# A planner's condition on the first layer's output weights, and new draws for its order

## The chip, the cores and the metric

The kernel runs on one core of one Trainium2 chip. The metric is device time in microseconds (us); the kernel before takes 1172.25 us as the median of 3 runs (1171.01 to 1172.92). The core has five engines that run their own instruction streams side by side: PE (TensorE, matmuls), DVE (VectorE), ACT (ScalarE), POOL (GpSimd) and SP (SyncE), which here issues the DMA transfers.

## The reference

Three steps follow one another: attention with pooled keys and values, a first layer with a softmax gate and a normalisation, and a second layer with a sigmoid gate. The inputs arrive as float64 words.

```python
k_p = k.reshape(B, H, Sp, pool, D).mean(axis=3)      # B = H = 8, S = 576, D = 64, pool = 8
v_p = v.reshape(B, H, Sp, pool, D).mean(axis=3)
attn = softmax(scale * q @ k_p.T)
x = (attn @ v_p) as (4608, 512)

h = x @ w_in                                         # 512 -> 1024
solu = h * softmax(h)
ln = (solu - mean(solu)) / sqrt(var(solu) + 1e-06) * g_ln
y = ln @ w_out                                       # 1024 -> 512

h = y @ w2_in                                        # 512 -> 2048
out = (h * sigmoid(1.702 * h)) @ w2_out              # 2048 -> 512
```

## The kernel before

The work has two phases. The first runs from the start to about 517 us: attention and the first layer over 36 tiles of 128 tokens, and besides, in the gaps, the preparation of all weights. The second phase, the remaining 652 us, is the second layer over 6 blocks of 768 tokens; its order is written out by hand.

In the first phase a planner (class `Plan`) sets the order. Each piece of work is a strand, a generator that yields operations (`Op`), requests for a tile (`New`) or conditions (a function that must give true before the strand goes on). In `Plan.run` the planner looks at the next operation of each strand, estimates when it could begin on its engine, adds a term from the strand's due time and a random number times a size, and emits the operation with the lowest score. `DRAWS` (line 85) lists up to which planned PE time which size and which seed hold. So one random stream decides between operations that are nearly equally good, and once one choice differs, all later draws meet other candidates. The emitted order is fixed at build time. Each engine executes its instructions in that order and waits at each for its inputs.

The strands that matter here:

- `w_in_part` (684) and `w_in_scale` (703): the four quarters of w_in are loaded (1 MB each, float64), their maximum is taken on DVE (tile `w1i_am`), spread over the partitions with a small matmul (`largest`, 566), and a power-of-two scale is computed from it (`whole_scale`, 645). Then `first_half` (670) writes each piece as a high half (ACT) and a low half (DVE) into `w1i`. The spread of an early scale uses the PSUM bank `psy`, of which there is one, shared with the pooled keys and values (`pooled`, 790) and with the projection.
- `second_weight` (718): w_out in four parts (`part`, 731). Each takes one of the 4 `raw` tiles, loads 1 MB, is joined to float32 (`joined`, 655: a sign and a scaling on ACT, a shift-and-or on DVE, a product on POOL) and measured (tile `w1o_am`). When all four are measured, the scale follows, and then the halves into `w1o`. The strands of w_in's last two quarters take their `raw` tiles first, so w_out's parts 2 and 3 wait until those give theirs back.
- `attention` (857): for each tile the scores (`psx`), softmax, and the softmax weights as high and low halves in `st`. A DMA transpose turns them into `aT`. For the first 4 tiles (`ALONE`) each transpose is issued by itself; `turned[t]` is set right after the planner has emitted it (lines 914 to 920). Then comes the product with the values (bank `psv`, of which there is one), and its halves go to `xT`.
- `Pair.hidden` (962): the product with w_in into `psh` (two buffers), its maximum, exponential, and the product with it (tile `tt`), which releases the buffer. `Pair.norm` (1008) ends with a DMA transpose into `zT`, and `Pair.project` (1050) multiplies with `w1o`.
- `Quarter` (1083) and `unit_scale` (1154): the second layer's weights, prepared in the same way in the gaps, from the time when the third tile's hidden product has been planned.

All loads, stores and transposes of this phase go through SP's queue, in the planner's order. An instruction there that waits for its input holds back those behind it.

Of the kernel before, what the change touches and what calls it, by code (L numbers as in the profile page):

```python
# [81 lines left out]
LATE = 3000  # L82
LATE_TURN = 3000
TTS = 4
DRAWS = ((70e3, 600, 13), (200e3, 150, 4), (330e3, 150, 13), (1e9, 150, 1))
V_TOP = 2.0 ** 14

TOP3 = 2.0 ** -29 * (1 - 2.0 ** -23)
# [95 lines left out]
class Plan:  # L184
# [7 lines left out]
    def __init__(self):  # L192
        self.free = dict.fromkeys(("pe", "dve", "act", "pool", "sp", "dma", "none"), 0.0)
        self.uses, self.floor, self.rings, self.ring_of = {}, {}, {}, {}
        self.strands, self.now, self.warm, self.pool_from = [], None, 0.0, 0.0
        self.draws = [(until, size, random.Random(seed)) for until, size, seed in DRAWS]

    def start(self, steps, due):
        s = Strand(self, steps, due)
        self.strands.append(s)  # L200
        return s
# [14 lines left out]
    def drop(self, *tiles):  # L216
        for t in tiles:
            del self.ring_of[t.name]
# [78 lines left out]
def moe_kernel(ctx: ExitStack, tc: tile.TileContext, qT, kT, vT, w_in, w_out, g_ln, w2_in, w2_out, eye, outT):  # L297
# [66 lines left out]
    class Tokens:  # L364
# [26 lines left out]
        def largest(self, diag):  # L391

            am = t1("yam")
            nc.vector.tensor_reduce(out=am, in_=self.two, axis=AX.X, op=ALU.max)
            nc.vector.tensor_scalar(out=diag, in0=eye_t, scalar1=am, scalar2=TINY, op0=ALU.mult, op1=ALU.max)
            self.diag = diag
# [39 lines left out]
    with ExitStack() as ph:  # L436
# [22 lines left out]
        def until(*strands):  # L459
            return lambda: all(s.ended for s in strands)  # L460
# [50 lines left out]
        def V(name, *args, **kw):  # L511
            return op(("dve",), name, args, kw)
# [47 lines left out]
        def s1(name, n=1, bufs=2):  # L560
            return small.tile([P, n], F32, name=name, tag=name, bufs=bufs)

        def absmax_op(dst, src, axis=AX.X):
            return V("tensor_reduce", out=dst, in_=src, axis=axis, op=ALU.max, apply_absolute_value=True)
# [68 lines left out]
        def raw_new(q, n):  # L633
            return New(kv, [P, q, n, 2], I32, "raw", "raw", RAWS)

        def raw_load(raw, src, i, n, q):
            return D(
                raw.rearrange("p q f t -> p q (f t)"),
                src[i * q * P : (i + 1) * q * P, :].bitcast(I32).rearrange("(q p) f -> p q f", p=P),
            )  # L640

        def high_words(raw):
            return raw[:, :, :, 1].bitcast(F32)

        def whole_scale(alln, up, dn):

            pw, rc = s1("pw", 1, KM), s1("rc", 1, KM)
            yield from exponent(pw, alln)
            yield V("reciprocal", rc, pw)
            yield V("tensor_scalar_mul", rc, rc, rc)  # L650
            yield V("tensor_scalar_mul", rc, rc, rc)
            yield V("tensor_scalar", out=up, in0=rc, scalar1=rc, scalar2=2.0 ** 8, op0=ALU.mult, op1=ALU.mult)
            yield V("reciprocal", dn, up)

        def joined(raw, measured):

            hw, lw = raw[:, :, 1], raw[:, :, 0]
            sg = yield New(kv, [P, 2 * WC], F16, "sgw", bufs=SG // 2)
            yield A(out=sg, in_=hw.bitcast(F32), func=AF.Sign)
            yield A(out=lw.bitcast(U32), in_=lw.bitcast(U32), func=AF.Copy, scale=TOP3, bias=-0.49999)  # L660
            yield measured
            yield A(out=hw.bitcast(F32), in_=hw.bitcast(F32), func=AF.Copy, scale=2.0 ** -112)
            yield V(
                "scalar_tensor_tensor", out=lw, in0=hw, scalar=3, in1=lw, op0=ALU.logical_shift_left,
                op1=ALU.bitwise_or,
            )
            yield G("tensor_tensor", out=lw.bitcast(F32), in0=sg, in1=lw.bitcast(F32), op=ALU.mult)
            drop(sg)

        def first_half(join, raw, scaled, up, k, c, his):  # L670

            yield join.over
            yield scaled
            word = raw[:, :, 0].bitcast(F32)
            hi, lo = (x[:, k, c] for x in his)
            yield A(out=hi, in_=word, func=AF.Copy, scale=up)
            yield V("scalar_tensor_tensor", out=lo, in0=word, scalar=up, in1=hi, op0=ALU.mult, op1=ALU.subtract)
# [40 lines left out]
        def second_weight(due):  # L718
            n = 4
            am, a1, alln, gs = s1("w1o_am", n), s1("w1o_a1"), s1("w1o_all"), s1("w1o_gs", K1)  # L720
            measured = [None] * n

            def scale():
                yield lambda: all(measured)
                yield V("tensor_reduce", out=a1, in_=am, axis=AX.X, op=ALU.max)
                yield from largest(a1, alln, WIDE_LEAST)
                yield from whole_scale(alln, w1o_up, w1o_dn)
                yield g_done.over
                yield V("tensor_scalar_mul", gs, g_col, w1o_up)

            def part(i):
                raw = yield raw_new(2, DM)
                yield raw_load(raw, w_out, i, DM, 2)
                join = start(joined(raw.rearrange("p q f t -> p (q f) t"), lambda: measured[i]), due + 4 * i)
                two = [
                    start(
                        first_half(
                            join, raw[:, j], scaled.over, gs[:, 2 * i + j : 2 * i + j + 1], 2 * i + j,
                            slice(0, WC), w1o,
                        ),  # L740
                        due + 4 * i,
                    )
                    for j in range(2)
                ]

                def measure():
                    yield absmax_op(am[:, i : i + 1], high_words(raw), axis=AX.XY)
                    measured[i] = True

                start(measure(), DUE_MAX_OUT)  # L750
                yield until(*two)
                drop(raw)

            scaled = start(scale(), due)
            yield until(*[start(part(i), due + 4 * i) for i in range(n)])

        BY_PRODUCT = (1, 2)
# [513 lines left out]
        q_loaded, scored, turned, valued, hid = ([False] * NTILE for _ in range(5))  # L1271
# [453 lines left out]
```

## Time and profile before

| | value |
|---|---|
| median of 3 runs | 1172.25 us |
| lowest, highest | 1171.01, 1172.92 us |
| the profiled execution | 1171.01 us |
| its span, first to last instruction | 1169.0 us |
| PE busy in the span | 1125.7 us (96%) |
| ACT, DVE, POOL busy | 754.7, 724.4, 617.7 us |
| mean granted PE clock | 0.994 of full speed |

The times below are microseconds from the span's start. Busy time of an engine leaves out waits and the issuing of DMAs. The granted clock is a share of 2.4 GHz: 1.00 is 2.4 GHz, 0.50 is 1.2 GHz, and a value between is a mean over a stretch that had both. DMA share is the mean busy share of the 16 transfer engines (overlapping transfers can bring it above 1). Idle time of PE is what to look at: it is the engine that is nearly always busy.

### The profile page before, as it was taken

Reading aid. Unit: us, or ns where it says so; the run is one execution under the profiler, and the core shown is the slowest. Engines: PE = TensorE matmul, PEld = TensorE weight load, DVE = VectorE, ACT = ScalarE, POOL = GpSimd, SP = SyncE. Lnnn points to the kernel's source line nnn. Section 1 sums busy time; section 2 is a strip of 40 time slices with the busy share of each in tenths; the row PEclk is TensorE's granted clock in tenths of the full one; section 3 lists DMA queues with packets and bytes.
Section 4 is the critical chain, followed back from the end, with each engine's and each line's share of the span. In section 5 each row is a group of like instructions: output and inputs, shape, how many; then the busy total and the mean of one; then the engine's idle time right before and its main releaser. Section 6 shows DMA issues by size and latency. Waiting matters only on the chain.

```text
span 1169.0 us, 19696 instructions
## 1 busy us (share of the span) xinstructions
PE 1125.7 (96%) x7737; PEld 726.1 (62%) x7737; DVE 724.4 (62%) x1105; ACT 754.7 (65%) x997; POOL 617.7 (53%) x643
## 2 busy tenths in 40 slices
PE   4888999999999999999999999999999999999998
PEld 4555676667676667765566656666666665566655
DVE  7988888777677753426753773567266636753650
ACT  6889998989798874737624752674367337625740
POOL 4566999989999985315503530561056016403530
PEclk9989999999999999999999999999999999999999
DMA  9979999999999768355465355536453653463131
GB/s 356 277 191 278 243 280 282 278 275 273 270 244 226 178 172 262 85 195 193 146 200 174 125 176 163 180 127 202 142 174 126 214 178 127 149 202 117 60 121 60
DMA packets 247356, 225.75 MB, mean 193 GB/s; under 512 B 165728, under 2 KB 218080, under 8 KB 246752
## 3 DMA queue, kind: packets, MB, share of 16 engines
q1 hardware_dynamic: 247264, 224.50, 67.0%
q8 instruction: 60, 0.98, 0.3%
q14 instruction: 32, 0.26, 0.1%
HBM read 151.06 MB, written 33.55 MB: 158 GB/s over the span
## 4 chain that ended last, share of the span: by engine, by line
PE 69%; POOL 13%; ACT 6%; DVE 5%; DMA 5%; issue 2%; SPq 1%; POOLq 0%; ACTq 0%; DVEq 0%
PE bank_a L1385 31%; PE bank_d L1385 16%; PE bank_b L1385 8%; PE psy L537 6%; PE psh L537 5%; POOL w_f L496 3%; PE psv L537 2%; POOL lo L496 2%; POOL zs L496 2%; POOL st L496 1%; POOL e L496 1%; PE psx L537 1%; DMA w2i_dram<-lo 1%; POOL q L496 1%; DMA raw<-w_out 1%
## 5 line engine op out<-in xcount | busy, mean ns | idle before, releaser
L1385 PEld LDWEIGHTS <-w2o 128*128 128x128 f16 x2016 | 197.0, 98 | 130.4
L1385 PEld LDWEIGHTS <-w2i 128*128 128x128 f16 x1974 | 193.1, 98 | 129.9 <-issue 2.4
L349 POOL TENSOR_TENSOR w_g<-w_g 128x384 f32<-128x384 f32 x42 | 46.1, 1097 | 399.2 <-ACT w_g L1464 399.2
L1479 DVE SCALAR_TENSOR_TENSOR g<-w_g,gu_b,g 128x1152 f16<-128x1152 f32 (+1 forms) x96 | 175.4, 1828 | 92.0 <-ACT g L1474 91.7
L1385 PE MATMUL bank_a<-ys,w2i 128*128 128x384 f16 x1128 | 205.6, 326 | 0.9 <-ACT c L1404 0.9
L537 PE MATMUL psh<-w1i,xT 128*128 128x512 f16 x864 | 201.8, 384 | 3.5 <-ACT xT L496 3.1
L1385 PE MATMUL bank_a<-g,w2o 128*128 128x384 f16 x1152 | 201.6, 326 | 0.0
L537 PEld LDWEIGHTS <-w1o 128*128 128x128 f16 x1728 | 168.0, 98 | 30.8 <-DMA zT<-zs 2.8
L537 PE MATMUL psy<-zT,w1o 128*128 128x256 f16 x1536 | 176.2, 273 | 3.5 <-DMA zT<-zs 2.3
L1474 ACT ACTIVATE g<-w_g,gu_b 128x1152 f16<-128x1152 f32 (+1 forms) x96 | 134.3, 1411 | 50.3 <-POOL w_g L352 39.3
L1404 ACT ACTIVATE c<-bank_a 128x384 f32<-128x384 f32 x188 | 90.7, 483 | 102.4 <-PE bank_a L1385 101.8
L537 PEld LDWEIGHTS <-xT 128*128 128x128 f16 x864 | 83.4, 99 | 96.3 <-issue 6.0
L1385 PE MATMUL bank_d<-g,w2o 128*128 128x384 f16 x576 | 104.2, 326 | 0.0
L496 POOL TENSOR_TENSOR zs<-tt,zs 128x1024 f16<-128x1024 f32 x36 | 78.4, 2178 | 44.2 <-ACT zs L496 43.8
L1385 PE MATMUL bank_d<-ys,w2i 128*128 128x384 f16 x564 | 101.1, 326 | 0.0
L1464 ACT ACTIVATE w_g<-c,ch_b 128x1536 f32<-128x1536 f32 x47 | 73.8, 1570 | 28.7 <-DVE c L1407 28.7
L352 POOL TENSOR_TENSOR w_g<-w_g 128x384 f32<-128x384 f32 x42 | 83.2, 1982 | 0.0
L1407 DVE SCALAR_TENSOR_TENSOR c<-bank_d,c 128x384 f32<-128x384 f32 x94 | 51.9, 552 | 41.9 <-ACT c L1404 29.6
L496 POOL TENSOR_TENSOR lo<-w_f,hi 128x512 f16<-128x512 f32 (+1 forms) x48 | 65.8, 1389 | 6.6 <-ACT e L496 2.9
L496 DVE TENSOR_REDUCE hmx<-psh 128x1 f32<-128x1024 f32 x36 | 43.8, 1218 | 36.2 <-PE psh L537 36.2
L537 PE MATMUL psx<-kbd,qt 128*128 128x144 f32 (+1 forms) x320 | 47.8, 312 | 15.1 <-ACT kbd L496 9.6
L496 DVE CUSTOM_DVE_ANT_0 tt<-psh,he 128x1024 f32<-128x1024 f32 x36 | 43.8, 1218 | 23.1 <-ACT he L496 22.9
(205 smaller groups left out, 1606.8 us busy)
## 6 DMA issues: line engine op xcount, KB each, us to landing
w2i<-w2i_dram SPq DMA_DIRECT2D x48, 896.0 KB, 4.6
w2o<-w2o_dram SPq DMA_DIRECT2D x84, 512.0 KB, 3.7
half<-kT SPq DMA_DIRECT2D x16, 576.0 KB, 6.4
half<-vT SPq DMA_DIRECT2D x16, 576.0 KB, 6.2
qt<-qT SPq DMA_DIRECT2D x36, 256.0 KB, 4.7
y_dram<-y SPq DMA_DIRECT2D x36, 256.0 KB, 3.5
y<-y_dram SPq DMA_DIRECT2D x48, 192.0 KB, 4.0
raw<-w_in SPq DMA_DIRECT2D x16, 512.0 KB, 7.7
```

The lines of the kernel that those rows point to most:

```text
L349: eng.tensor_tensor(out=w[:, 1], in0=q[:, Q12], in1=q[:, Q11], op=ALU.subtract)
L352: eng.tensor_tensor(out=w[:, 3], in0=q[:, Q21], in1=w[:, 2], op=ALU.subtract)
L496: getattr(eng, name)(*args, **kw)
L537: nc.tensor.matmul(*p[:3], start=p[3], stop=p[4], skip_group_check=len(p) > 5)
L1385: nc.tensor.matmul(bank, self.weight(p, kk, w), self.data(p, kk, i), start=(first and kk == 0 and w == 0 and i == 0), stop=(last and kk == ...
L1404: nc.scalar.activation(out=self.c[:, i], in_=getattr(self, bank), func=AF.Copy, scale=self.scale)
L1407: nc.vector.scalar_tensor_tensor(out=self.c[:, i], in0=getattr(self, bank), scalar=self.scale, in1=self.c[:, i], op0=ALU.mult, op1=ALU.add,)
L1464: nc.scalar.activation(out=self.w[:, 0:4], in_=self.c, func=AF.Gelu_apprx_sigmoid, scale=self.ch)
L1474: nc.scalar.activation(out=self.g[s.start][:, 0], in_=self.w[:, s], func=AF.Copy, scale=self.gu)
L1479: nc.vector.scalar_tensor_tensor(out=self.g[s.start][:, 1], in0=self.w[:, s], scalar=self.gu, in1=self.g[s.start][:, 0], op0=ALU.mult, op1 ...
```

## The change

A condition is added at the head of each part of `second_weight`: the part asks for its tile, and so issues its load, only once the planner has emitted the first tile's transpose. And `DRAWS` gets other seeds and other borders: one seed up to 70 us of planned PE time as before, one up to 280 us in place of two up to 330 us, and one for the rest; the sizes are as before.

```diff
-DRAWS = ((70e3, 600, 13), (200e3, 150, 4), (330e3, 150, 13), (1e9, 150, 1))
+DRAWS = ((70000.0, 600, 23), (280000.0, 150, 23), (1000000000.0, 150, 491854))
...
             def part(i):
+                yield lambda: turned[0]
                 raw = yield raw_new(2, DM)
                 yield raw_load(raw, w_out, i, DM, 2)
                 join = start(joined(raw.rearrange("p q f t -> p (q f) t"), lambda: measured[i]), due + 4 * i)
```

## Rows read from the trace of the kernel before

**Rows 1.** The page: busy us of each engine, share of the span, instructions.

```profile
PE 1125.7 (96%) x7737; PEld 726.1 (62%) x7737; DVE 724.4 (62%) x1105; ACT 754.7 (65%) x997; POOL 617.7 (53%) x643
```

**Rows 2.** Stretches: length; busy PE, PEld, DVE, ACT, POOL; clock; DMA share; GB/s.

```profile
0.00:36.06 36.06, 14.81 (x83) 13.26 (x83) 26.29 (x47) 25.16 (x35) 18.63 (x25) 1.00 0.99 338
36.06:65.50 29.44, 29.44 (x209) 19.43 (x210) 28.50 (x49) 24.42 (x33) 15.70 (x14) 0.94 1.05 276
65.50:102.00 36.50, 28.62 (x188) 17.89 (x186) 33.08 (x74) 32.99 (x54) 22.63 (x33) 0.91 0.86 216
...
130.00:517.00 387.00, 378.23 (x3070) 267.31 (x3068) 251.18 (x461) 306.65 (x444) 313.76 (x377) 1.00 0.92 229
517.00:1169.00 652.00, 647.65 (x3979) 388.76 (x3977) 360.65 (x433) 339.73 (x399) 224.42 (x168) 1.00 0.46 155
```

**Rows 3.** PE in order of time: start, us, instruction [idle before <-releaser].

```profile
30.25 0.22 PE L537 MATMUL psy<-diag,ones 128*128 128x128 bf16 x1 [2.06 <-ACT kp L496]
...
36.06 2.59 PE L537 MATMUL psh<-w1i,xT 128*128 128x512 f16 x6 [3.12 <-ACT xT L496]
...
69.07 0.22 PE L537 MATMUL psy<-diag,ones 128*128 128x128 bf16 x1 [2.41 <-ACT kp L496]
71.40 0.27 PE L537 MATMUL psy<-diag,ones 128*128 128x128 bf16 x1 [2.11 <-DVE mean L496]
...
102.08 5.41 PE L537 MATMUL psy<-zT,w1o 128*128 128x256 f16 x48 [2.34 <-DMA zT<-zs]
```

**Rows 4.** Short stretches, columns as in rows 2.

```profile
24.00:26.00 2.00, 2.00 (x10) 2.00 (x10) 2.00 (x4) 2.00 (x5) 0.93 (x1) 1.00 1.04 406
26.00:28.00 2.00, 2.00 (x18) 2.00 (x17) 2.00 (x5) 2.00 (x3) 0.69 (x1) 1.00 1.36 104
70.00:78.00 8.00, 6.60 (x23) 3.96 (x23) 5.67 (x24) 5.20 (x9) 5.80 (x13) 0.57 0.83 176
300.00:308.00 8.00, 5.90 (x65) 4.12 (x65) 6.30 (x19) 5.39 (x8) 7.77 (x15) 0.79 1.12 302
```

**Rows 5.** DVE in order of time, 30 to 71 us.

```profile
30.99 1.21 DVE L496 TENSOR_REDUCE w1o_am<-raw 128x1 f32<-128x1024 f32 x1
32.12 0.14 DVE L496 TENSOR_SCALAR pw<-w1i_all 128x1 int32<-128x1 int32 x1
...
59.09 1.21 DVE L496 TENSOR_REDUCE w1o_am<-raw 128x1 f32<-128x1024 f32 x1
...
62.14 1.22 DVE L496 SCALAR_TENSOR_TENSOR raw<-raw 128x1024 int32<-128x1024 int32 x1
...
64.66 2.02 DVE L496 SCALAR_TENSOR_TENSOR raw<-raw 128x1024 int32<-128x1024 int32 x1
...
69.92 1.22 DVE L496 CUSTOM_DVE_ANT_0 tt<-psh,he 128x1024 f32<-128x1024 f32 x1
```

**Rows 6.** SP's issues in order of time, 18 to 51 us.

```profile
18.99 0.43 SPq L528 DMA_DIRECT2D raw<-w_out  x1
22.82 5.03 SPq L528 DMA_TRANSPOSE aT<-st  x1
...
31.30 1.06 SPq L528 DMA_DIRECT2D raw<-w_out  x1
...
50.41 0.38 SPq L528 DMA_DIRECT2D raw<-w_out  x1
```

**Rows 7.** ACT in order of time, 26 to 34 us.

```profile
26.84 0.40 ACT L496 ACTIVATE diag<-eye_t,w1i_a 128x128 bf16<-128x128 f32 x1
...
32.49 1.11 ACT L496 ACTIVATE sgw<-raw 128x1024 f16<-128x1024 f32 x1
```

**Rows 8.** Writers of w1o: count, ns least/median/most, first and last start.

```profile
L496 DVE SCALAR_TENSOR_TENSOR w1o<-raw,w1o_gs,w1o x8: 743/744/746, 78.1 to 82.8; 128x512 f16<-128x512 f32 x8
```

**Rows 9.** PE after 130 us: the two longest waits, columns as in rows 3.

```profile
226.75 0.64 PE L537 MATMUL psv<-aT,vst 128*64 128x128 f16 x16 [1.68 <-DVE xT L496]
...
302.10 0.83 PE L537 MATMUL psv<-aT,vst 128*64 128x64 f16 x32 [2.20 <-DVE w2all L496]
```

## The prediction

> **What bounds the kernel now.** I read the page's busy line first, then the table of stretches, then TensorE's waits (PE), and last the other engines around each wait. PE is busy 1125.7 us of a span of 1169.0 us [rows 1], so 43.3 us of idle time is all that an order can win back at full clock. The table says where it lies [rows 2]: 36.06 − 14.81 = 21.25 us before the first hidden product, none from 36.06 to 65.5, 36.5 − 28.62 = 7.9 us from 65.5 to 102, 387 − 378.2 = 8.8 us from 130 to 517, and 4.35 us in the 652 us after it. That last stretch is written out by hand and isn't drawn, so I leave it as it is. From 36 to 102 us the reader should see VectorE (DVE): 28.5 of 29.4 us and 33.1 of 36.5 us [rows 2]. There the vector work sets the pace; after 130 us PE does.
>
> The largest loss in one place is at 65.5 to 78 us: PE waits 2.41 us and at once 2.11 us more [rows 3], and then works at half clock. The granted clock over 70 to 78 us is 0.57 [rows 4], so it stood at 1.2 GHz for 8 × 0.43 × 2 = 6.9 us. About 1.1 us of these lie in the wait itself; the other 5.8 us do half of what they could, which is 2.9 us lost. So this hole costs 4.5 + 2.9 = 7.4 us. DVE never rests ahead of it, and of its work from 59 to 70 us three pieces are w_out's: 1.21, 1.22 and 2.02 us [rows 5], 4.45 us in all, queued in front of the reduction at 69.92 us that frees the bank for the next hidden product.
>
> **The moved load.** Of the four w_out loads of 1 MB, the sync queue (SP) issues one at 18.99 us, ahead of the first transpose of softmax weights at 22.82 us, and the next at 31.30 us; the other two come later, the last at 50.41 us [rows 6]. So three of the four already obey the new condition. Part 0 is the only one that it must move, to behind 22.82 + 5.03 = 27.85 us, 9 us or more later. No instruction is added: the condition holds back the planner's strand and puts no semaphore wait on any engine. What moves with part 0 are its DMA, its maximum on DVE (1.21 us at 30.99), its sign on ScalarE (ACT, 1.11 us at 32.49) and all that follows; they pass the transposes and loads that SP issues from 22.82 to 31.30.
>
> What this gives in front: the spread for w_in's scale runs on PE at 30.25 us [rows 3], and a next step of that scale, at 32.12, stands on DVE right behind part 0's maximum [rows 5]. ACT then does part 0's sign at 32.49 ahead of the first w1i pieces [rows 7]. Either removal lets the chain to the first hidden product at 36.06 us [rows 3] go 1.1 to 1.2 us sooner; they are in series with different engines and the second shrinks behind the first, so I take −1.1 us once. Bounds: 0, if another step is drawn into the gap, and −4.1 us, if the spread for w_in's scale also loses its wait: its diagonal is ready at 26.84 + 0.40 = 27.24 us [rows 7], but the product runs at 30.25, as its bank is held by pooled keys until ACT has copied them out [rows 3]. Those 3.0 us belong to the draw, not to the condition, and I count none of them.
>
> What the DMA gives: from 24 to 26 us plain loads still move at 406 GB/s, and at 26 to 28 the rate drops to 104 with the transfer engines fully busy, which is the transpose at work [rows 4]. So the transpose issued at 22.82 waits for about 1.05 MB / 406 GB/s = 2.6 us of part 0. The first turned tile can be there up to 2.6 us earlier. I count nothing for it: the first hidden product waits for ACT and the scale chain above. If that cover goes (scale early, ACT free), it is what allows the −4.1 us; there it is no further term.
>
> What it costs: part 0's DVE work leaves a stretch that has room (26.3 of 36.06 us) and comes back between 36 and 102 us, where DVE is full [rows 2]. I take +1.2 us for the maximum. Bounds: 0, if it displaces a step that can wait until after 130 us, where DVE works 251 of 387 us, and +2.0 us, the longest w_out step in that stretch [rows 5]. Its ACT work finds 5 us of room from 36 to 65.5 [rows 2] and costs nothing; without that room it would be 1.1 us. The two terms, −1.1 and +1.2, all but cancel: by itself the condition is worth nothing that can be seen.
>
> A rule of the Trainium skill speaks against it. "DMA: Bandwidth & Descriptors", section Rules for kernel authors, advises to issue a DMA early, compute meanwhile and wait for it late. By it w1o would be ready later, and every microsecond beyond the slack would be lost. The slack here: the last w1o pieces start at 82.8 us and take 0.74 [rows 8], while the first product with w1o runs at 102.08 and waits for its other operand, the transposed zT [rows 3]. That is 18.5 us against a move of 9 to 12, so by the trace the price is 0. It stays a rival.
>
> **The redrawn order.** New seeds change every choice up to 517 us, not only this load, and the trace of before shows no row of the new order. I bound it by the old holes. The big one is a coincidence: two spreads next to each other in PE's order, behind three w_out steps on DVE. A new order may have it whole (0) or not at all (−7.4 us); I take half, −3.7 us. The small ones after 130 us sum to 8.8 us, the largest 2.20 and 1.68 us [rows 9]; as many can come as go: 0. For the spread of that zero I take the two largest as drawn or not: sqrt(2.20² + 1.68²) = 2.8 us either way.
>
> **Sum.** −1.1 + 1.2 − 3.7 = −3.6 us. The profiled execution took 1171.01 us (2.0 us around its span) and is the fastest of three; it gives 1167.4 us. The median, 1172.25, lies 1.24 us above it, so I forecast 1168.6 us.
>
> **The rivals.**
> - Hidden anyway. Three of four loads stand where they should, PE waits for DVE and not for DMA, and the new order has a hole of its own as dear as the old one. Then −1.1 + 1.2 remains: 1172.3, say 1171 to 1174 us. For it: the order of causes at 36 to 102 us, where DVE is full in any order.
> - Everything falls right. The spread of w_in no longer waits 3.0 us, and the hole at 65.5 us closes whole: −1.1 − 3.0 + 1.2 − 7.4 = −10.3 us, 1162.0 us. Against it: DVE stays full there, so the hole should reappear in part.
> - Slower, by holes in the stretch where PE sets the pace. PE there waits for the single bank psv, behind DVE: 1.68 us for the attention's low half, 2.20 us for a maximum of second-layer weights [rows 9]; after the second the clock is 0.79 over 300 to 308 us [rows 4], 1.7 us more. If the new order has one more of each, it loses 1.68 + 2.20 + 1.7 = 5.6 us, and if the hole at 65.5 us stays as well, that makes −1.1 + 1.2 + 5.6 = +5.7: 1178.0 us. It decides once these new holes exceed what the front gives back by 2.3 us. For it: from 130 to 517 us PE is busy 97.7% now, so there is more to lose than to win.
> - Slower, by the page's rule: w1o too late. If the remaining parts slip behind part 0, each by its 9 to 12 us, twice that is 18 to 24 us: up to 24 − 18.5 = 5.5 us past the slack, 1177.8 us. It decides beyond 20.8 us of delay. Against it: parts 2 and 3 wait for tiles that w_in's parts 2 and 3 give back, and not for part 0.
>
> **How the numbers follow.** Chances: the forecast 0.40, everything right 0.12, hidden anyway 0.22, slower by holes 0.20, slower by a late w1o 0.06. About 0.2%, 2.3 us, is what a measurement of this kernel can tell from no change, so the bounds are 1169.9 and 1174.6 us. Faster: 0.40 + 0.12 = 0.52; same: 0.22; slower: 0.20 + 0.06 = 0.26. The likeliest case has its own range of 1165 to 1169.9 us. The range for 8 in 10 runs from the best case, 1162.0, to just under the slower ones, 1177.5: it leaves out half of the best case and half of the slower ones, 0.19.
>
> **What the profile of the changed kernel would show.** Right: the first w_out load behind the first transpose on SP; no w_out maximum between the steps of w_in's scale; the first hidden product at 35 us or earlier; less than 4.5 us of PE waits between 60 and 80 us and a clock above 0.57 there; from 130 to 517 us some 9 us idle; the hand-written stretch again 652 us long. Wrong: a first hidden product at 36 us or later (the front's step fails); PE waiting for w1o's pieces at its first use rather than for zT (the rule was right); more than 12 us idle between 130 and 517 us, or new half-clock stretches there (the rival by holes); a last stretch that differs by over 1 us, which no step of mine explains.

## The result: 1.3% slower, all of it lost in the planned phase

The changed kernel takes 1188.07 us (median of 6 runs, 1185.06 to 1192.97) against 1172.65 us for the kernel before, measured beside it (1171.01 to 1177.64). The ratio is 1.0126 [1.0107, 1.0144]. The forecast was 1168.6 us, with a range of 1162.0 to 1177.5.

The page of the changed kernel, busy us of each engine, to be set beside [rows 1]; its span is 1186.3 us:

```profile
PE 1124.2 (95%) x7737; PEld 724.1 (61%) x7737; DVE 737.9 (62%) x1108; ACT 753.5 (64%) x990; POOL 614.3 (52%) x641
```

TensorE has the same work (1124.2 against 1125.7 us), so what is lost is idle time: 1186.3 − 1124.2 = 62.1 us against 43.3. Where it lies shows the table of stretches of the changed kernel (columns as in [rows 2]; the hand-written part begins at 531.93 us here, at 514.20 before):

```profile
0.00:39.50 39.50, 18.06 (x115) 16.89 (x115) 28.86 (x49) 25.22 (x34) 21.15 (x25) 0.96 0.95 311
39.50:79.70 40.20, 36.50 (x283) 23.37 (x283) 39.10 (x79) 35.99 (x54) 23.47 (x27) 1.00 0.84 227
79.70:104.00 24.30, 15.65 (x83) 8.93 (x82) 19.73 (x39) 23.66 (x37) 16.78 (x19) 0.79 1.02 232
104.00:130.00 26.00, 20.55 (x184) 15.39 (x183) 18.46 (x38) 19.69 (x30) 19.12 (x21) 0.89 1.10 227
130.00:531.93 401.93, 383.54 (x3084) 269.04 (x3082) 270.33 (x473) 307.45 (x438) 309.44 (x383) 0.99 0.91 224
531.93:1186.30 654.37, 649.93 (x3997) 390.49 (x3994) 361.41 (x434) 341.47 (x401) 224.29 (x168) 1.00 0.47 157
```

Length minus TensorE's busy time gives the idle time: 21.4 us up to the first hidden product (before: 21.25, [rows 2]), 3.7 + 8.65 + 5.45 = 17.8 us from there to 130 us (before 8.9 from 36.06 to 130), 18.4 us in the rest of the planned phase (before 8.8), and 4.4 us in the hand-written part (before 4.35). So the front and the end are as they were. The middle loses 8.9 + 9.6 us.

TensorE's wait before the first hidden product and its longest waits after it in the changed kernel, columns as in [rows 3]:

```profile
39.50 0.61 PE L537 MATMUL psh<-w1i,xT 128*128 128x512 f16 x2 [0.69 <-ACT xT L496]
86.12 2.26 PE L537 MATMUL psx<-kbd,qt 128*128 128x144 f32 x8 [6.40 <-issue]
90.63 1.06 PE L537 MATMUL psv<-aT,vst 128*64 128x128 f16 x16 [2.25 <-DVE xT L496]
127.55 1.06 PE L537 MATMUL psv<-aT,vst 128*64 128x128 f16 x16 [5.39 <-DMA aT<-st]
152.94 2.78 PE L537 MATMUL psy<-zT,w1o 128*128 128x256 f16 x24 [2.11 <-ACT y L496]
198.43 0.22 PE L537 MATMUL psv<-diag,ones 128*128 128x128 bf16 x1 [3.43 <-DVE xT L496]
344.45 0.64 PE L537 MATMUL psv<-aT,vst 128*64 128x128 f16 x16 [2.78 <-DVE xT L496]
412.36 5.40 PE L537 MATMUL psy<-zT,w1o 128*128 128x256 f16 x48 [2.65 <-ACT y L496]
```

The old hole at 65.5 to 78 us is gone: over 60 to 80 us TensorE is busy 18.39 of 20 us at clock 1.00 (columns as in [rows 2]):

```profile
60.00:80.00 20.00, 18.39 (x151) 12.12 (x149) 19.32 (x42) 18.94 (x27) 14.92 (x17) 1.00 0.60 144
```

In its place stand two holes, 6.40 + 2.25 us at 80 to 91 us (clock 0.50 over 84 to 92) and 5.39 us at 122 us (0.52 over 124 to 130).

The first hole read from VectorE, in order of time (start, us, instruction):

```profile
73.93 2.19 DVE L496 SCALAR_TENSOR_TENSOR w1o<-raw,w1o_gs,w1o 128x512 f16<-128x512 f32 x1
...
77.85 0.74 DVE L496 SCALAR_TENSOR_TENSOR w1o<-raw,w1o_gs,w1o 128x512 f16<-128x512 f32 x1
...
78.64 4.05 DVE L496 SCALAR_TENSOR_TENSOR w1o<-raw,w1o_gs,w1o 128x512 f16<-128x512 f32 x6
...
83.27 1.21 DVE L496 CUSTOM_DVE_ANT_0 tt<-psh,he 128x1024 f32<-128x1024 f32 x1
...
84.41 0.75 DVE L496 TENSOR_REDUCE mx<-psx 128x8 f32<-128x576 f32 x1
...
85.26 0.76 DVE L496 TENSOR_TENSOR e<-psx,mx 128x576 f32<-128x576 f32 x1
```

All eight low halves of w1o stand between 73.9 and 82.7 us, 7 us of work, six of them in one lump, in front of the steps that empty `psx`; TensorE's next scores start when `e` has read it. Such a lump alone makes no hole, though. In the kernel before all eight stand in one lump too, and TensorE, which had hidden products and pooled keys and values to work on meanwhile, waited for nothing from 72 to 86 us:

```profile
78.13 5.38 DVE L496 SCALAR_TENSOR_TENSOR w1o<-raw,w1o_gs,w1o 128x512 f16<-128x512 f32 x8
```

The second hole read from SP's queue:

```profile
29.41 2.73 SPq L528 DMA_TRANSPOSE aT<-st  x1
...
32.82 0.42 SPq L528 DMA_DIRECT2D raw<-w_out  x1
...
106.53 11.97 SPq L528 DMA_TRANSPOSE zT<-zs  x2
...
121.06 6.25 SPq L528 DMA_TRANSPOSE aT<-st  x2
```

A pair of `zT` transposes holds the queue for 12 us, and the softmax weights for which TensorE waits are turned behind it. The first two lines show the change itself: the first w_out load is issued after the first transpose, as the condition asks.

### The profile page after: what moved, and what is told of

It reads as the page before. It is cut to its first block, busy times and chain, and to the rows that moved or that the text cites. A ratio compares the mean times of both kernels' runs of the same rounds, so it can differ in the third digit from the quotient of the medians.

```text
span 1186.3 us, 19709 instructions
## 1 busy us (share of the span) xinstructions
PE 1124.2 (95%) x7737; PEld 724.1 (61%) x7737; DVE 737.9 (62%) x1108; ACT 753.5 (64%) x990; POOL 614.3 (52%) x641
## 4 chain that ended last, share of the span: by engine, by line
PE 66%; POOL 11%; ACT 7%; DMA 6%; DVE 5%; issue 3%; SPq 1%; POOLq 0%; ACTq 0%; DVEq 0%
PE bank_a L1386 31%; PE bank_d L1386 15%; PE bank_b L1386 8%; PE psy L537 6%; PE psh L537 4%; POOL w_f L496 3%; DMA aT<-st 3%; PE psv L537 2%; POOL zs L496 2%; POOL lo L496 2%; ACT he L496 1%; DMA half<-vT 1%; ACT st L496 1%; POOL st L496 1%; POOL e L496 1%
## 5 line engine op out<-in xcount | busy, mean ns | idle before, releaser
L537 PE MATMUL psh<-w1i,xT 128*128 128x512 f16 x864 | 202.4, 385 | 1.5 <-DVE w1i L496 0.8
L537 PEld LDWEIGHTS <-w1o 128*128 128x128 f16 x1728 | 168.2, 98 | 33.8 <-issue 8.1
L537 PE MATMUL psy<-zT,w1o 128*128 128x256 f16 x1584 | 181.1, 273 | 5.2 <-ACT y L496 5.2
L537 PEld LDWEIGHTS <-xT 128*128 128x128 f16 x864 | 82.8, 99 | 96.2 <-issue 9.9
L496 POOL TENSOR_TENSOR zs<-tt,zs 128x1024 f16<-128x1024 f32 x36 | 77.9, 2166 | 39.4 <-ACT zs L496 39.2
L537 PE MATMUL psx<-kbd,qt 128*128 128x144 f32 (+1 forms) x320 | 45.9, 304 | 25.6 <-ACT raw_z L496 13.3
L496 POOL TENSOR_TENSOR lo<-w_f,hi 128x512 f16<-128x512 f32 (+1 forms) x46 | 62.2, 1364 | 14.0 <-DMA w2i_dram<-lo 9.3
L496 DVE TENSOR_REDUCE hmx<-psh 128x1 f32<-128x1024 f32 x36 | 43.8, 1218 | 34.3 <-PE psh L537 34.3
L537 PEld LDWEIGHTS psx<-kbd,qt 128*128 128x128 f32 (+1 forms) x320 | 41.2, 191 | 35.2 <-issue 17.9
```

Of the source, the lines that this page charges most:

```text
L496: getattr(eng, name)(*args, **kw)
L537: nc.tensor.matmul(*p[:3], start=p[3], stop=p[4], skip_group_check=len(p) > 5)
```

## Experiments

Each edit is shown against the kernel that it starts from. "Order replayed" means that the planner's choices are replaced by a list, recorded from the named kernel, of which strand emits its next operation on which engine; a move is then an edit of that list and nothing else shifts. In those kernels the same lines have other numbers: L590 is L528, L599 or L598 is L537, and L558 or L557 is L496. Ratios are to the kernel before, run beside it on the same chip.

### The condition without a new draw

The order of before is replayed; only w_out's first part moves:

```diff
 # order of before, recorded
-SP   load raw<-w_out, part 0            (18.99 us)
 SP   transpose aT<-st
 SP   transpose vst<-vx
+SP   load raw<-w_out, part 0
 ...  # its ACT sign moves to just ahead of its scaling, its DVE maximum to just ahead of part 1's
```

> The order of before, replayed step by step from a list, with only what the condition asks for: the first w_out load goes behind the first softmax-weight transpose (and the first transpose of values), its sign to just before its scaling on ACT, its maximum to just before the next w_out maximum on DVE. Everything else keeps its place. Theory D: 1170 to 1175 us, within 0.3% of before, with the first hidden product about 1 us earlier than 36.06. Theory C: 1180 us or more.

Measured: 1172.31 us, ratio 1.0003 [0.9988, 1.0019]. SP's and TensorE's rows of this kernel, to be set beside [rows 6] and [rows 3]:

```profile
22.64 1.87 SPq L590 DMA_TRANSPOSE aT<-st  x1
...
26.50 0.57 SPq L590 DMA_DIRECT2D raw<-w_out  x1
```

```profile
34.80 1.61 PE L599 MATMUL psh<-w1i,xT 128*128 128x512 f16 x6 [2.83 <-ACT xT L558]
...
60.29 1.46 PE L599 MATMUL psh<-w1i,xT 128*128 128x512 f16 x6 [1.29 <-DVE mean L558]
70.12 0.27 PE L599 MATMUL psy<-diag,ones 128*128 128x128 bf16 x1 [2.84 <-ACT kp L558]
72.38 0.27 PE L599 MATMUL psy<-diag,ones 128*128 128x128 bf16 x1 [1.99 <-DVE mean L558]
```

The transpose no longer waits for part 0 (1.87 us of issue in place of 5.03). The first hidden product starts at 34.80 in place of 36.06 us, so 1.26 us sooner. At 60.29 there is a wait of 1.29 us behind VectorE that the trace of before doesn't have. What the front gives, the full stretch takes back: the condition by itself is worth nothing that the median of 10 runs shows. The trace agrees in the two places only. It is of a run of 1174.11 us; TensorE idles 11.6 us from 130 us to the hand-written part (8.8 before), which begins at 517.5 in place of 514.2 us. Whether the edit has a part in that or this execution was a long one, a single trace can't tell.

The reverse, in the order of the changed kernel replayed, puts the first w_out load back to the front:

```diff
 # order of the changed kernel, recorded
+SP   load raw<-w_out, part 0            (about 17 us)
 SP   transpose aT<-st
-SP   load raw<-w_out, part 0            (32.82 us)
```

> The order of the changed kernel, replayed step by step, with only the first w_out load put back to the front (behind the load of the gains, at about 17 us, ahead of the first transpose). Theory D: 1184 to 1192 us, as the changed kernel. Theory C: most of the loss is gone, 1178 us or less.

Measured: 1185.02 us, 1.0109 [1.0087, 1.0132]. The interval overlaps that of the changed kernel (1.0126 [1.0107, 1.0144]), and the hole at 80 to 91 us is still there (4.73 + 2.25 us). Where that load stands isn't the cause.

### Each half of the edit, drawn anew

```diff
 # first kernel: old seeds, the condition alone
             def part(i):
+                yield lambda: turned[0]
 # second kernel: no condition, the new seeds alone
-DRAWS = ((70e3, 600, 13), (200e3, 150, 4), (330e3, 150, 13), (1e9, 150, 1))
+DRAWS = ((70000.0, 600, 23), (280000.0, 150, 23), (1000000000.0, 150, 491854))
```

> The condition alone, with the seeds of before. The stream of random numbers meets other candidates from the second step on, so this too is a new order. Theory D (the loss comes from drawing the order anew, whatever the condition): slower than before by some 5 to 25 us, 1178 to 1198 us, with holes at other places than in the changed kernel. Theory C (the later load itself costs the time): 1185 to 1192 us, with the same holes near 80 and 122 us.

> The new seeds alone, without the condition: again a new order. Theory D: 1178 to 1198 us. Theory C: the loss is gone, 1168 to 1176 us.

Measured: 1193.01 us, 1.0178 [1.013, 1.0226], and 1190.87 us, 1.0159 [1.0125, 1.0194]. Either half alone costs as much as both. With the old seeds the condition still makes a new order, because the planner meets other candidates and the random stream then lands on other choices. Against the kernel above, whose condition leaves the order as it was, that is 1.0178 against 1.0003 for the same edit.

So other draws were run, three of the kernel before (seeds 1, 101, 201, 301; 6, 106, 206, 306; 10, 110, 210, 310; sizes and borders of before) and two with the condition (seeds 1, 101, 201, 301; 3, 103, 203, 303).

> The kernel before with four other seeds (1, 101, 201, 301) and no condition. Theory D (any fresh draw falls short of the order of before): 1176 to 1205 us. If the order of before is an ordinary one: 1166 to 1178 us.

> The kernel before with seeds 6, 106, 206, 306 and no condition. Theory D: 1176 to 1205 us. If the order of before is an ordinary one: 1166 to 1178 us.

> The kernel before with seeds 10, 110, 210, 310 and no condition. Theory D: 1176 to 1205 us. If the order of before is an ordinary one: 1166 to 1178 us.

> The condition with seeds 1, 101, 201, 301. Theory D: 1176 to 1205 us, no worse as a group than the draws without the condition. Theory C (the condition costs time): above all draws without it.

> The condition with seeds 3, 103, 203, 303. Theory D: 1176 to 1205 us, no worse as a group than the draws without the condition. Theory C: above all draws without it.

| freshly drawn order | us | ratio |
|---|---|---|
| new seeds, no condition | 1190.87 | 1.0159 [1.0125, 1.0194] |
| seeds 1, ... | 1190.05 | 1.0153 [1.0114, 1.0192] |
| seeds 6, ... | 1191.78 | 1.0157 [1.0078, 1.0237] |
| seeds 10, ... | 1182.10 | 1.0097 [1.0062, 1.0131] |
| changed kernel | 1188.07 | 1.0126 [1.0107, 1.0144] |
| old seeds, condition | 1193.01 | 1.0178 [1.013, 1.0226] |
| seeds 1, ..., condition | 1194.04 | 1.0177 [1.01, 1.0254] |
| seeds 3, ..., condition | 1188.90 | 1.0133 [1.0072, 1.0194] |

All eight are slower than the old order, by 0.97 to 1.78%. The four without the condition have a mean of 1188.7 us, the four with it 1191.0; the groups overlap, and whether those 2.3 us are the condition's stays open. The old order is the exception, not the changed one. How its seeds were found isn't on record. If they were picked from many by their time, that eight others are slower is what one would expect; no run shows it.

### Closing the two holes by hand

In the order of the changed kernel, replayed. The first kernel takes the lump of w1o halves apart, the second lets the turn pass `zT`, the third does both:

```diff
 # first: ahead of the hole at 80 us
+ACT, DVE  xT of the fifth tile, and its hidden product on PE    (sooner)
-DVE  w1o low halves, seven of the eight                         (moved behind it)
-SP   two loads of second-layer weights                          (moved behind it)
 # second: on SP
+SP   transpose aT<-st x2
 SP   transpose zT<-zs x2
-SP   transpose aT<-st x2
```

> The order of the changed kernel, replayed, with one place rewritten: near 80 us the first hidden factor (xT of tile 4) goes on ACT and DVE ahead of the normalisation steps, the hidden product that needs it follows at once on PE, and seven low halves of w1o (and the two second-layer loads that need their tiles) go behind the scores' work on DVE. Theory H (the loss is made of single holes that local steps put in PE's way): the 6.4 and 2.3 us waits near 80 and 90 us and the half clock after them shrink to under 4 us together, and the kernel takes 1177 to 1182 us. Rival S (DVE and ACT are short of time in the whole stretch from 40 to 130 us, so a hole that is closed opens again a little later): 1184 to 1188 us, with new waits between 92 and 130 us.

> The order of the changed kernel, replayed, with one thing moved on SP's queue: the transposes of softmax weights issued at 121 us go ahead of the two transposes of normalised hidden values issued at 106.5 us. Theory H: the wait of 5.4 us at 122 us shrinks to under 2 us and the kernel takes 1181 to 1185 us. Rival S: 1185 to 1190 us, since the second projection waits for the values that now come later.

> Both edits of the order of the changed kernel. Theory H: the gains add up, 1171 to 1179 us. Rival S: 1183 to 1189 us.

Measured: 1191.21 us (1.016 [1.0139, 1.0181]), 1184.12 us (1.0113 [1.0089, 1.0136]) and 1192.57 us (1.0175 [1.0159, 1.0191]). TensorE's waits in the first and then in the second:

```profile
81.87 1.46 PE L599 MATMUL psh<-w1i,xT 128*128 128x512 f16 x6 [2.00 <-DVE mean L558]
85.50 1.22 PE L599 MATMUL psx<-kbd,qt 128*128 128x144 f32 x8 [2.17 <-issue]
91.81 2.26 PE L599 MATMUL psx<-kbd,qt 128*128 128x144 f32 x8 [3.13 <-DVE e L558]
...
112.33 0.27 PE L599 MATMUL psv<-diag,ones 128*128 128x128 bf16 x1 [6.14 <-ACT diag L558]
```

```profile
86.51 2.26 PE L599 MATMUL psx<-kbd,qt 128*128 128x144 f32 x8 [4.76 <-issue]
...
150.44 5.28 PE L599 MATMUL psy<-zT,w1o 128*128 128x256 f16 x24 [5.12 <-ACT y L558]
```

In the first, one hole of 6.40 us becomes several of 2 to 3 us and one of 6.14 at 112 us. In the second, the hole at 122 us is gone and one of 5.12 us opens at 150 us, where the projections now wait; what is left is a gain of about 4 us in the median, 1.5 us by the ratios, whose interval overlaps that of the changed kernel. The median of the second lies in the range of theory H all the same; the first and the third came out above the ranges of both theories. So closing these holes one by one moved them.

### How much of the old order has to be kept

No condition; the seeds of before hold up to 70, 200 or 330 us of planned TensorE time, others behind (the 200 us border twice, with different seeds):

```diff
-DRAWS = ((70e3, 600, 13), (200e3, 150, 4), (330e3, 150, 13), (1e9, 150, 1))
+DRAWS = ((70e3, 600, 13), (200e3, 150, 101), (330e3, 150, 201), (1e9, 150, 301))  # kept to 70
+DRAWS = ((70e3, 600, 13), (200e3, 150, 4), (330e3, 150, 201), (1e9, 150, 301))    # kept to 200
+DRAWS = ((70e3, 600, 13), (200e3, 150, 4), (330e3, 150, 206), (1e9, 150, 306))    # kept to 200, again
+DRAWS = ((70e3, 600, 13), (200e3, 150, 4), (330e3, 150, 13), (1e9, 150, 301))     # kept to 330
```

> Order and seed of before up to 70 us of planned TensorE time, other seeds behind it, no condition. The four orders drawn wholly anew without the condition have, against before, this much less TensorE busy time on average: 1.5 us at 0 to 36 us, 0.3 at 36 to 70, 3.5 at 70 to 130, 3.8 at 130 to 200, 0.9 at 200 to 330, 4.9 at 330 to 514. Theory E (every part of the old order is better than a draw, and each part costs its own): the first 1.8 us are kept, the rest is lost: about 1185 us, 1180 to 1189. Theory F (the first 70 us decide: a bad order there leaves debts of weights and tiles that are paid later): within 3 us of before, 1170 to 1176.

> Order and seeds of before up to 200 us of planned TensorE time, other seeds behind it, no condition. Theory E: 0.9 + 4.9 = 5.8 us are lost: about 1178 us, 1174 to 1182. Theory F': the stretch up to 200 us decides, and what follows is as good in any draw: 1171 to 1174.

> As the one with the order of before up to 200 us, with other seeds behind it. Theory E: about 1178 us, 1174 to 1182, and not far from the other. Theory F': 1171 to 1174.

> Order and seeds of before up to 330 us of planned TensorE time, another seed behind it, no condition. Theory E: 4.9 us are lost: about 1177 us, 1174 to 1180. Theory F': 1171 to 1174.

| kept up to | us | ratio |
|---|---|---|
| 70 us | 1190.40 | 1.0172 [1.0145, 1.0198] |
| 200 us | 1177.83 | 1.0052 [1.0033, 1.0071] |
| 200 us, other seeds | 1179.94 | 1.0076 [1.0056, 1.0096] |
| 330 us | 1174.49 | 1.0016 [0.9999, 1.0033] |

The first 70 us of the old order save nothing: with them kept, the loss is as large as with none (1.0172 against 1.0097 to 1.0159). Keeping it up to 200 us brings back 0.96 to 1.2% (11 to 14 us), up to 330 us a further 0.36 to 0.6%; what is behind 330 us costs 0.16%, which the interval doesn't tell from nothing. Theory F fell, and so did theory F' for the orders kept to 200 us (1171 to 1174 us). Theory E was right in kind, but had only 7.3 us for 70 to 200 us, and the order kept to 70 us came out just above its range (1180 to 1189 us). The stretches of 70 to 130 and 130 to 200 us in the kernel before, then in the one kept to 70 us, then in the one kept to 200 us (columns as in [rows 2]):

```profile
70.00:130.00 60.00, 54.22 (x393) 36.28 (x393) 53.31 (x113) 54.41 (x80) 40.72 (x59) 0.94 0.99 247
130.00:200.00 70.00, 69.00 (x579) 48.61 (x577) 55.69 (x102) 61.82 (x90) 67.17 (x77) 1.00 1.06 271
```

```profile
70.00:130.00 60.00, 47.15 (x360) 31.74 (x361) 47.94 (x106) 48.95 (x76) 34.44 (x53) 0.94 0.99 221
130.00:200.00 70.00, 68.05 (x566) 46.15 (x561) 52.90 (x102) 62.84 (x91) 64.67 (x72) 1.00 1.07 268
```

```profile
70.00:130.00 60.00, 52.19 (x375) 34.65 (x375) 51.84 (x112) 52.53 (x78) 38.93 (x57) 0.94 1.00 241
130.00:200.00 70.00, 68.59 (x580) 48.60 (x579) 57.13 (x103) 61.59 (x92) 67.32 (x74) 1.00 1.03 266
```

Up to 200 us the first and the third kernel have the same order, so 52.19 for 54.22 us is scatter between executions; 47.15 lies well outside it (the other two kernels kept to 200 us or more have 53.94 and 53.49). In the order kept to 70 us, TensorE is busy 8.0 us less than before from 70 to 200 us and 10.7 us less from 200 to 514 us; in the one kept to 200 us, with the same seeds behind, it is 2.3 us less from 200 to 514 us. So a worse choice between 70 and 200 us is paid for in part later, or the same seeds pick worse there because they meet other candidates; these runs don't separate the two.

Between 70 and 130 us this worse order leaves every engine with less to do: TensorE 47.15 for 54.22 us, but also VectorE 47.94 for 53.31, ScalarE 48.95 for 54.41, GpSimd 34.44 for 40.72. None of the four is full there; that they wait for one another in turn is how I read it, and not shown. The transfer engines are full in both (DMA share 0.99, 247 and 221 GB/s), but in the eight fresh orders of the whole phase their share in this stretch is 0.85 to 1.05, so being full there isn't what the slow ones have in common.

### The bank that is freed late

From 36 us to the hand-written part TensorE waits for the single bank `psv` behind VectorE's `xT` this long (total us, times, longest), before and then changed:

```profile
PE psv L537 <- DVE xT L496: 4.6, 6, 1.7
```

```profile
PE psv L537 <- DVE xT L496: 11.5, 5, 3.4
```

In the other seven fresh orders it is 10.8 to 20.5 us. To see whether this is the cause, the two steps that copy `psv` into `xT`, and the second-layer maxima that hold the bank, were pulled forward on their engines as far as the plan allows, in the orders of the changed kernel and of before. `xT` got a third buffer for it; the pull and the buffer weren't tried apart:

```diff
-            xT = yield New(sb, [P, 2 * KM, P], F16, "xT", bufs=2)
+            xT = yield New(sb, [P, 2 * KM, P], F16, "xT", bufs=3)
 # order recorded; for each product into psv:
+ACT  xT high half, then DVE xT low half, ahead of work planned behind the product's end
```

> The order of the changed kernel with one thing pulled forward: wherever the plan allows it, the two steps that copy a product of weights and values out of the single bank psv (ScalarE's high half and VectorE's low half into xT) and the maxima of second-layer weights that hold it go ahead of the other work of their engines; so that they can, xT gets three buffers in place of two. From 36 us to the hand-written part TensorE waits for psv behind VectorE's xT 11.5 us in the changed kernel, 4.6 in the one before, 10.8 to 20.5 in the other fresh orders. Theory P (this bank, freed late, is what a fresh order loses by): most of the difference of 6.9 us comes back, 1179 to 1183 us, with at most 6 us of such waits in the trace. Theory W (an order's holes are not one resource's; what is pulled forward pushes other steps back): 1185 us or more, with the waits for psv shorter and others longer.

> The same pull and the third xT buffer in the order of the kernel before, which has 4.6 us of such waits left. Theory P: 2 to 4 us are won, 1168 to 1170.5 us. Theory W: no gain, 1171 to 1175 us.

Measured: 1187.66 us, 1.0112 [1.0091, 1.0132], in the order of the changed kernel, and 1170.12 us, 0.9959 [0.994, 0.9977], in that of before. The waits in the first of the two:

```profile
PE psx L598 <- issue: 8.9, 2, 6.4
PE psy L598 <- ACT y L557: 7.3, 8, 2.4
PE psv L598 <- DVE xT L557: 3.7, 3, 1.9
```

The waits behind `xT` fall from 11.5 to 3.7 us, below those of the old order, and the hand-written part starts at 529.7 in place of 531.9 us. Of 7.8 us, 2.2 arrive. The waits for `psx` grow from 7.7 to 8.9 and those for ScalarE's `y` from 5.2 to 7.3 us. So theory P falls for the changed order: the bank is where the lateness shows, not what makes it. In the old order the same edit gives the only version that beats both kernels, by 0.41%, in the range that theory P gave; its trace shows the waits at 2.2 us for 4.6 and the hand-written part at 513.5 for 514.2 us, so 0.7 us of this gain has a place in the trace. The rest hasn't, and the kernel before took 1175.35 us beside these two, against 1171.6 to 1172.7 beside all others; so I read it as a small gain of uncertain size.

## Why the prediction was wrong, step by step

**The moved load** was right in both terms. −1.1 us in front measured −1.26, +1.2 us behind measured +1.29 as a new wait on VectorE, and the DMA's part (3.2 us less of issue for the first transpose) was hidden, as said. Their sum was taken as nothing; alone it measured 1.0003 [0.9988, 1.0019].

**The rule to issue early and wait late** (the Trainium skill, "DMA: Bandwidth & Descriptors", Rules for kernel authors) speaks against the change. Here the trace shows neither a loss nor a gain by it: in the changed kernel TensorE first uses w1o at 104.23 us without a wait for it, and the same load late or early in one order is within 0.2%.

**The redrawn order** is the step that failed. It took half of the big hole, −3.7 us, because a new order may have it whole or not at all, and for the small ones "as many can come as go: 0", with 2.8 us either way. The big hole did vanish from its place, more than was forecast. But the sum of holes didn't stay: +8.9 us from the front to 130 us, that gain already deducted, and +9.6 us from there to the hand-written part. The error is in taking the old order as a typical one, around which a new draw scatters evenly. Eight draws lie 10 to 22 us above it and none below. By them the term was +16 us without the condition (1188.7 − 1172.65), with some 4 us of scatter between draws.

**The rival by holes in the stretch where TensorE sets the pace** had the sign and the sentence that mattered: at 97.7% busy [rows 2] there is more to lose than to win. It got a chance of 0.20 and a price of 5.6 us, two holes of the old order's own size. The new ones behind 130 us number four of over 2 us, the largest 3.43, and no rival had new holes before 130 us dearer than the old one, where 14 us came in three waits.

**VectorE sets the pace from 36 to 102 us** was read off a busy share of 91 to 97% in the old order [rows 2]. From 36 to 102 us it is as full in the changed kernel (61.4 of 66 us, 61.6 before), but in the other seven fresh orders it is at 54.5 to 60.0 us, and TensorE does less there in all eight (51.7 to 57.5 us, 58.1 before). So how full VectorE is doesn't tell the good order from the bad ones, and a share near full in one order doesn't say that the engine has no room in another.

**The signs.** Right were the load behind the first transpose, no w_out maximum between the steps of w_in's scale (the first comes at 43.77 us, that scale is done at 33.3), no wait for w1o, the old hole's place (18.39 us busy of 20 from 60 to 80 us) and the hand-written stretch (654.4 us, and 654.2 to 655.0 in every kernel here). The sign "first hidden product at 36 us or later" was ill chosen: it came at 39.50 us, with the same idle time before it, because 3.25 us of other TensorE work had been drawn ahead (18.06 for 14.81 us). "More than 12 us idle behind 130 us, new half-clock stretches" is the one that fired. The half clock isn't where the difference lies: TensorE's busy sum, which holds what it stretches, is no longer than before.

**What stays open:** by which trait an order is good. The choices between 70 and 200 us matter most, by the runs with a part of the old order kept; it isn't the place of the w_out load, not the two largest holes, and not the late bank, each by itself. Whether the condition costs 2 us in a typical draw is open too.

## What to carry to other kernels

Where a planner breaks near-ties with random numbers, any edit that it can see draws the whole order anew, and the draw is then what is measured. To price the edit, replay the old order and move only the edit's own steps; to price the redraw, run several seeds without the edit and see where the old order lies among them before assuming that gains and losses cancel. Here TensorE was busy 97.7% behind 130 us in the old order, and eight fresh draws of eight lost against it.

## What the runs showed of the hardware

VectorE has 13.5 us more busy time in the changed kernel, with three more instructions. In part it was given other ones, in part the same ones took longer. One form that reads two tiles, `st` minus its high half, runs once on VectorE in the kernel before (0.80 us) and three times here (7.9 us in all). Before, then in the changed kernel, with what GpSimd (POOL) ran at that time:

```profile
404.43 0.80 DVE L496 TENSOR_TENSOR st<-e,st 128x576 f16<-128x576 f32 x1
403.88 1.94 POOL L496 TENSOR_TENSOR w_f<-w_f 128x256 f32<-128x256 f32 x2
```

```profile
303.08 5.41 DVE L496 TENSOR_TENSOR st<-e,st 128x576 f16<-128x576 f32 x1 [0.82 <-POOL zs L496]
303.00 2.78 POOL L496 TENSOR_TENSOR lo<-w_f,hi 128x512 f16<-128x512 f32 x2
305.72 2.16 POOL L496 TENSOR_TENSOR zs<-tt,zs 128x1024 f16<-128x1024 f32 x1
```

In the changed kernel the VectorE instruction starts 0.08 us behind GpSimd's first and ends 0.6 us behind its third. The Trainium skill, "SBUF — State Buffer", section SBUF: two separate sides, says that GpSimd and a VectorE instruction with two inputs in SBUF share a pair of ports, that whichever starts first has it for its whole instruction, and that the other is blocked. The trace of the changed kernel agrees in that VectorE, which started second, took 5.41 us in place of 0.80, and it shows more: the blocked one stood back for three instructions in a row, not for one. That isn't always so. In the kernel before, the same VectorE instruction also began while GpSimd ran two back to back and took its 0.80 us; there GpSimd's two took 1.94 us, where single ones of this form beside them take 0.72 and 0.73. What decides who goes next isn't shown. TensorE was busy in every one of the 5.4 us, so this one cost nothing at that moment. That such stretching is what makes fresh orders slow isn't shown: the best of them has 248.6 us of VectorE time behind 130 us, less than the old order's 250.1.
